# Weight words handled in the mask-bit steps, and the first pair's mask bits by fp32 products in column tiles

## The chip, the cores and the metric

The kernel runs on one core of a Trainium2 chip. The metric is the device time of one execution in microseconds (us). A program's time holds its span (first to last instruction) and a little around it.

## What is computed

Sixteen heads of masked attention (2 batches, 8 heads, 768 positions, width 64) are followed by two dense feed-forward blocks over the 1536 tokens. Everything comes and goes as fp32; the feed-forward weights arrive as 64-bit words and are turned into fp32 on the chip.

```python
q_bits = (q @ proj > 0); k_bits = (k @ proj > 0)       # 6 bits for each position
mask   = bucket(q_bits)[:, None] == bucket(k_bits)[None, :]
scores = where(mask, scale * q @ k.T, -1e9)
attn   = softmax(scores);  x = attn @ v                # per head
h = relu(x @ w_in);   x = (h * h) @ w_out              # 1536 x 512 -> 2048 -> 512
h = x @ w2_in;        y = (h * sigmoid(h)) @ w2_out
```

## The kernel before

**Attention.** The heads go in eight pairs. A pair has four units (head 0 or 1, query half z 0 or 1 of 384 columns), a unit has three score tiles of 128 queries by 768 keys. Each loop step `d`, from -5 to 98, handles one score tile and two transposed tiles:

- TensorE transposes two finished 128-key slices of the probabilities (`transp`, three 128x128 pieces each, tiles `t`), multiplies two older slices with v (`av`, two products each, tile `o`), then makes the next score tile (`score_mm`, four products, tile `s`).
- ScalarE rounds the transposed tiles (`t_hi`, tiles `th`) and takes the exponentials (`score_exp`).
- VectorE takes the row maximum of the score tile made one step earlier (`row_max`, L983), two tiny operations on it (`row_live`), and the remainders of the transposed tiles (`t_lo`, L1023, tiles `tl`), whose end gives a `t` buffer back. There are three `t` buffers and two `s` buffers.

Operations in `mid[d]` are put on VectorE right behind `row_live` of step `d`; operations given by `at(d, ...)` are put at the end of step `d` on their engine. All engines run their own list in this order.

**fp32 by two rounded parts.** Fast products take rounded operands (fp32r). So q and k are split into a rounded part and a remainder: for later pairs GpSimd rounds (`cast_pair`, tiles `hq`, `hk`) and subtracts (`split_pair`, tile `lp`), and DMAs place the parts in the operand tiles `qq` and `kk` (`load_head`, `place_lo`).

**Mask bits.** Twelve extra rows of `qq` and `kk` carry the bits, so that a mismatch makes a score hugely negative. For pairs 1 to 7 the bits come from four fp32 products of 32 columns each, one in each quarter of the array (`bits_mm`), and one compare on VectorE (`bits_cmp`), placed by DMAs (`place_bits`). This is done in seven steps, called bits steps here: d = 1, 10, 22, 34, 46, 58, 70. In a bits step both `t_lo` of the step run before the products, and the compare comes in the next step. For pair 0, the lead-in, head 0 takes its bits from rounded parts against a split projection `pjd` (`first_bits_mm`, tiles `bf`), and head 1 from eight products at step -2 (`second_bits_mm`, tiles `bs`).

**First-block weights.** During attention four slices of w_in are converted from 64-bit words: ScalarE `w_abs`, GpSimd `w_limit`, then on VectorE `w_exp`, `w_sign`, `w_low` (L945, L949, L953), in `mid` of the last three steps of each row of `W_STEPS`; `wp_put` splits the first two on GpSimd.

**Feed-forward.** After step 98 a planner orders the two blocks; its table and rules are not touched, and its instruction order is the same in both kernels. TensorE is fed with zero products (`warm_up`, L967) before and inside the lead-in.

Of the kernel before, what the change touches and what calls it, by code (L numbers as in the profile page):

```python
# [26 lines left out]
QW = 384  # L27
# [4 lines left out]
WARM = {-4: 5, 0: 1, 1: 1}  # L32
# [8 lines left out]
W_STEPS = ((0, 5, 17, 29, 53), (8, 17, 41, 65, 77), (22, 29, 41, 92, 93), (54, 65, 92, 96, 96))  # L41
# [658 lines left out]
def lsh_attention_moe_moe(ctx, tc, kd, qk, qf, fq, v, pc, wi1, wo1, wi2, wo2, out):  # L700
# [28 lines left out]
    pjd = ac.tile([128, 3, 88], F32R, name="pjd")  # L729
    pdx = ac.tile([128, 2, NBR], F32, name="pdx")  # L730
# [67 lines left out]
    def first_load(h):  # L798
# [19 lines left out]
        if h == 0:  # L818
            first["hk", 0] = a1.tile([128, S], F32R, tag="hk", name="hk0_0")
# [16 lines left out]
    def first_k_hi(z, i):  # L836
        (nc.gpsimd.tensor_copy if i else nc.scalar.copy)(out=pair[0]["kk"][0][0:64, i, half(z)], in_=first[0, 1][z][0:64])

    def first_hk(z):
        nc.scalar.copy(out=first["hk", 0][64:128, half(z)], in_=first[0, 1][z][64:128])  # L840

    def first_k_lo(z):
        (nc.gpsimd if z else nc.vector).tensor_tensor(
            out=pair[0]["kk"][0][64:128, 0, half(z)], in0=first[0, 1][z][64:128], in1=first["hk", 0][64:128, half(z)].bitcast(F32), op=ALU.subtract
        )
# [13 lines left out]
    def first_ops(h, z):  # L859
        q, k, zs = pair[0]["qq"][h], pair[0]["kk"][h], half(z)  # L860
        up, dn, all_ = slice(0, 64), slice(64, 128), slice(0, 128)
        of_q = [(0, all_, q[:, 0, zs]), (0, up, q[up, 1, zs])]
        if h:
            return of_q, [(1, all_, k[:, 0, zs]), (2, up, k[up, 0, zs])]
        hk = first["hk", 0]
        return of_q, [(1, dn, hk[dn, zs]), (2, dn, hk[dn, zs]), (1, dn, k[dn, 0, zs])]

    def first_bits_mm(i, z):
        o = first["bits", i, z] = ps_t.tile([128, 512], F32, tag="t", name=f"bf{i}{z}")
        ops = first_ops(0, z)[i]  # L870
        for n, (w, rows_, x) in enumerate(ops):
            mm(o[0:76, 0:QW], pjd[rows_, w, 0:76], x, start=n == 0, stop=n == len(ops) - 1)
            if i + z + n == 0:
                warm_up(1)

    def first_bits_cmp(i, z, a=0, b=QW):
        m = tm[1 + i][64:76]
        nc.vector.tensor_scalar(
            out=pair[0][("qq", "kk")[i]][0][64:76, 1, half(z)][:, a:b], in0=first["bits", i, z][64:76, a:b],
            scalar1=m[:, 0:1], scalar2=m[:, 1:2], op0=ALU.is_gt, op1=ALU.mult,  # L880
        )


    def second_bits_mm(z):
        o = first["both", z] = ps_t.tile([128, 512], F32, tag="t", name=f"bs{z}")
        ops = [(64 - NBR * i, *first_ops(1, z)[i][n]) for i, n in ((1, 1), (0, 0), (1, 0), (0, 1))]
        for n, (c, w, rows_, x) in enumerate(ops):
            mm(o[0 : 2 * NBR, 0:QW], pjd[rows_, w, c : c + 2 * NBR], x, start=n == 0, stop=n == len(ops) - 1)

    def second_bits_cmp(z):  # L890
        if z == 0:
            first["bt"] = a1.tile([128, S], F32R, tag="bt", name="bt0")
        m = tm[3][0 : 2 * NBR]
        nc.vector.tensor_scalar(
            out=first["bt"][0 : 2 * NBR, half(z)], in0=first["both", z][0 : 2 * NBR, 0:QW], scalar1=m[:, 0:1], scalar2=m[:, 1:2], op0=ALU.is_gt, op1=ALU.mult
        )

    def second_place(n, zs):
        nc.sync.dma_start(
            out=pair[0][("qq", "kk")[n]][1][64 : 64 + NBR, 1, zs].bitcast(F32), in_=first["bt"][NBR * n : NBR * n + NBR, zs].bitcast(F32)  # L900
        )
# [210 lines left out]
    for p in range(1, NPAIR):  # L1112
        d0 = 12 * (p - 1)
        if p > 1:
            at(d0 - 10, load_pair, p)
            at(d0 - 9, load_k, p)
            at(d0 - 4, new_hi, p)
            at(d0 - 4, cast_pair, p, 1)
            at(d0 - 3, split_pair, p, 1)
            scale[d0 - 2] = p  # L1120
            at(d0 - 2, cast_pair, p, 0)
            at(d0 - 1, split_pair, p, 0)
# [5 lines left out]
        at(d0 + 2, place_lo, p, 0)  # L1128
# [22 lines left out]
    for i, (d_load, d_abs, *d_dve) in enumerate(W_STEPS):  # L1151
# [7 lines left out]
        if i < 2:  # L1159
            at(d0, wp_put, i)  # L1160
# [4 lines left out]
    with tc.manual_schedule():  # L1165
# [10 lines left out]
        warm_up(9)  # L1176
# [169 lines left out]
```

## Time and profile before

| | |
|---|---|
| median of 3 runs | 715.39 us (715.32 to 716.03) |
| profiled execution | 717.23 us, span 715.5 us |
| TensorE busy | 707.4 us (99%) |
| VectorE / ScalarE / GpSimd busy | 605.4 / 537.7 / 257.6 us |
| attention stage | to about 223 us of the span |
| an ordinary attention step | 2.05 to 2.06 us |
| a bits step with its products | 2.98 us |

In a timeline, each row has a start, a length and what was run; brackets show how long the engine sat idle before it and what ended that. Two VectorE rows may overlap by about 0.08 us, since one starts as the other drains. The distance of two score rows on TensorE is the length of a step.

### The profile page before, as it was taken

The numbers are of one execution on the slowest core, as the hardware profiler recorded it, in microseconds if no ns is written. First come the engines' busy times: TensorE is split into PE (matmuls) and PEld (weight loads), VectorE is DVE, ScalarE is ACT, GpSimd is POOL, SyncE is SP. The second block draws the span as 40 slices with busy tenths as digits, with TensorE's granted clock in tenths as the row PEclk, the third lists the DMA queues.
The fourth block names the chain that finished last, engine by engine and source line by source line (L and its number), as shares of the span: only waits on it lengthen the run. The fifth ranks groups of instructions, "written<-read, shape, count | busy, mean of one in ns | idle before, by whom it ended". The sixth has DMA issues, their size and how long they took to land.

```text
span 715.5 us, 10860 instructions
## 1 busy us (share of the span) xinstructions
PE 707.4 (99%) x3610; PEld 602.9 (84%) x3610; DVE 605.4 (85%) x1099; ACT 537.7 (75%) x1012; POOL 257.6 (36%) x239
## 2 busy tenths in 40 slices
PE   9999999999999999999999999999999999999998
PEld 4899999999998888888887888888888888888886
DVE  6999999999999879887897789988878778888840
ACT  6999999999997787594477469788765955854861
POOL 7546575657665221042231241245114011212300
PEclk9999999999999999999999999999999999999999
DMA  5778967967733455242534832487221332245432
GB/s 171 206 177 194 228 159 193 232 160 198 174 96 86 110 162 118 89 131 46 117 89 122 183 93 73 104 184 174 71 73 60 101 106 86 76 103 119 103 110 96
DMA packets 39495, 92.51 MB, mean 129 GB/s; under 512 B 5944, under 2 KB 11588, under 8 KB 39440
## 3 DMA queue, kind: packets, MB, share of 16 engines
q1 hardware_dynamic: 26976, 67.58, 31.6%
q0 software_dynamic: 12032, 23.79, 18.7%
q8 instruction: 28, 0.46, 0.3%
q10 hardware_dynamic: 432, 0.46, 0.2%
q14 instruction: 27, 0.22, 0.1%
HBM read 52.32 MB, written 3.19 MB: 78 GB/s over the span
## 4 chain that ended last, share of the span: by engine, by line
PE 87%; DVE 10%; issue 1%; DMA 1%; ACT 0%; DVEq 0%; ACTq 0%; POOLq 0%
PE bank L558 36%; PE bank L443 24%; PE bank L420 7%; PE s L976 6%; PE t L1012 6%; DVE mt L983 4%; DVE tl L1023 4%; PE o L1036 3%; PE o L1037 3%; DMA cell<-cell 1%; PE bs L786 1%; PE warm L967 1%; DVE mt L988 1%; DVE mt L987 0%; ACT P L996 0%
## 5 line engine op out<-in xcount | busy, mean ns | idle before, releaser
L558 PE MATMUL bank<-woh,cell 128*128 128x512 f32 (+1 forms) x392 | 119.8, 385 | 0.0
L558 PE MATMUL bank<-cell,woh 128*128 128x512 f32 x384 | 118.4, 389 | 1.1 <-DMA cell<-cell 1.1
L996 ACT ACTIVATE P<-s,mt 128x768 f32<-128x768 f32 x96 | 95.6, 995 | 13.5 <-DVE mt L988 11.7
L1023 DVE TENSOR_TENSOR tl<-t,th 128x384 fp32r<-128x384 f32 x192 | 104.0, 547 | 0.1
L983 DVE TENSOR_REDUCE mt<-s 128x1 f32<-128x768 f32 x96 | 91.3, 951 | 3.1 <-PE s L976 2.4
L558 PEld LDWEIGHTS bank<-cell,woh 128*128 128x128 f32 x384 | 72.1, 188 | 16.4 <-DMA cell<-cell 1.5
L558 PEld LDWEIGHTS bank<-woh,cell 128*128 128x128 f32 x392 | 73.1, 188 | 14.6
L1017 ACT CAST th<-t 128x384 fp32r<-128x384 f32 x192 | 82.2, 482 | 3.2 <-PE t L1012 3.0
L976 PE MATMUL s<-kk,qq 76*128 76x384 f32 (+1 forms) x384 | 83.4, 338 | 0.5 <-ACT P L996 0.3
L1012 PE MATMUL t<-ident,P 128*128 128x128 f32 x576 | 80.6, 273 | 1.8 <-DVE tl L1023 1.8
L1012 PEld LDWEIGHTS t<-ident,P 128*128 128x128 f32 x576 | 67.5, 140 | 11.3 <-DVE tl L1023 7.2
L278 DVE TENSOR_TENSOR cell<-bank,cell 128x512 f32<-128x512 f32 x91 | 62.1, 691 | 17.5 <-PE bank L443 13.1
L443 PE MATMUL bank<-xw,wpb 128*128 128x512 f32 x312 | 75.9, 389 | 0.0
L558 PE MATMUL bank<-wol,cell 128*128 128x512 f32 (+1 forms) x196 | 75.4, 385 | 0.0
L558 PE MATMUL bank<-cell,wol 128*128 128x512 f32 x192 | 74.7, 389 | 0.0
L1036 PE MATMUL o<-th,vv 128*128 128x384 f32 x192 | 72.7, 379 | 0.0
L976 PEld LDWEIGHTS s<-kk,qq 76*128 76x128 f32 (+1 forms) x384 | 67.9, 188 | 2.3 <-ACT P L996 1.6
L443 PEld LDWEIGHTS bank<-xw,wpb 128*128 128x128 f32 x312 | 58.5, 188 | 12.4 <-DVE bank L278 0.3
L1037 PE MATMUL o<-tl,vv 128*128 128x384 f32 x192 | 64.7, 337 | 0.0
L450 ACT COPY cell<-bank 128x512 f32<-128x512 f32 x39 | 22.9, 586 | 39.5 <-PE bank L443 37.5
L268 ACT CAST cell<-cell 128x512 fp32r<-128x512 f32 x81 | 48.8, 617 | 2.8 <-DMA cell<-cell 1.7
L271 POOL DMA_DIRECT2D cell<-cell x23 | 20.5, 906 | 82.4 <-ACT cell L270 59.4
(185 smaller groups left out, 1461.2 us busy)
## 6 DMA issues: line engine op xcount, KB each, us to landing
raw<-in_dram SPq DMA_DIRECT2D x62, 512.0 KB
cell<-cell POOLq DMA_DIRECT2D x23, 256.0 KB, 3.8
qq<-hq SPq DMA_DIRECT2D x28, 192.0 KB
kk<-in_dram POOLq DMA_DIRECT2D x14, 384.0 KB, 4.5
yf<-cell POOLq DMA_DIRECT2D x21, 256.0 KB, 3.6
vr<-in_dram SPq DMA_DIRECT2D x8, 384.0 KB
ta<-ob SPq DMA_DIRECT2D x31, 96.0 KB
tb<-ob SPq DMA_DIRECT2D x31, 96.0 KB
```

The costliest lines, as they stand in the source:

```text
L278: add("DVE", 0.70, lambda: vec.tensor_tensor(out=val(out), in0=bank[b], in1=val(other), op=ALU.add), [("bank", b), *reads], writes)
L420: mm(bank[b], wpa[n][:, p, 4 * h + j], x[:, q], start=j == 0 and z == 0, stop=j == 3 and z == 2)
L443: mm(bank[b], w[:, p], x[:, q], start=not started and z == 0, stop=z == 2, skip_group_check=started)
L558: mm(bank[b][:, 0:wd], x, y, start=start and i == 0 and z == 0, stop=i == (FB if half is None else 2 * half + 2) - 1 and z == 2, skip_grou ...
L976: mm(s[:, n, 0:QW], t["qq"][h][0:kk, ab, c0 : c0 + 128], t["kk"][h][0:kk, ab, n * QW : (n + 1) * QW], start=ab == 0, stop=ab == 1)
L983: nc.vector.tensor_reduce(out=m[:, 0:1], in_=s[:, :, 0:QW], op=ALU.max, axis=AX.XY, negate=True)
L996: nc.scalar.activation(out=e.rearrange("p (a b) -> p a b", a=2), in_=s[:, :, 0:QW], func=AF.Exp, scale=m[:, 1:2], bias=m[:, 2:3], accum_ou ...
L1012: nc.tensor.transpose(t[:, j * 128 : (j + 1) * 128], P[u, j][:, kt * 128 : (kt + 1) * 128], ident)
L1017: nc.scalar.copy(out=th, in_=PT[g][0][:, 0:QW])
L1023: nc.vector.tensor_tensor(out=tl, in0=t[:, 0:QW], in1=th.bitcast(F32), op=ALU.subtract)
L1036: mm(o[:, 0:QW], vv, th, start=kt == 0, stop=False)
L1037: mm(o[:, 0:QW], vv, tl, start=False, stop=kt == KT - 1)
```

## The change

It has two parts.

1. *Bits steps.* The VectorE operations of w_in slices 0 and 1 move from steps 17, 29, 53 and 41, 65, 77 to the bits steps 10, 22, 34 and 46, 58, 70; slice 2's first moves from 41 to 46. `wp_put` comes seven steps after the last of them. In pairs 2 to 7 GpSimd no longer rounds and splits k ahead of q: all four operations are put in the bits step, q first. `place_lo` of head 0 comes one step later.
2. *First pair.* The split projection `pjd` is gone. One fp32 matrix `pdz` is multiplied with the loaded q and k themselves, four products in column tiles for each head (at the start, and at step -4), head 1's compare is the common `bits_cmp` (step -2, instead of two compares in step -1) and its bits go out in four DMAs. Head 0's k is rounded in all 128 rows at once, straight into `kk`. Zero products: 7 instead of 9 at the start, 3 instead of 5 at step -4, one new at -2.

```diff
-WARM = {-4: 5, 0: 1, 1: 1}
+WARM = {-4: 3, -2: 1, 0: 1, 1: 1}
-W_STEPS = ((0, 5, 17, 29, 53), (8, 17, 41, 65, 77), (22, 29, 41, 92, 93), (54, 65, 92, 96, 96))
+W_STEPS = ((0, 5, 10, 22, 34), (8, 17, 46, 58, 70), (22, 29, 46, 92, 93), (54, 65, 92, 96, 96))
...
     def first_k_hi(z, i):
-        (nc.gpsimd.tensor_copy if i else nc.scalar.copy)(out=pair[0]["kk"][0][0:64, i, half(z)], in_=first[0, 1][z][0:64])
-
-    def first_hk(z):
-        nc.scalar.copy(out=first["hk", 0][64:128, half(z)], in_=first[0, 1][z][64:128])
+        kk, k = pair[0]["kk"][0], first[0, 1][z]
+        if i:
+            nc.gpsimd.tensor_copy(out=kk[0:64, 1, half(z)], in_=k[0:64])
+        else:
+            nc.scalar.copy(out=kk[:, 0, half(z)], in_=k)
...
-    def first_bits_mm(i, z):
-        o = first["bits", i, z] = ps_t.tile([128, 512], F32, tag="t", name=f"bf{i}{z}")
-        ops = first_ops(0, z)[i]
-        for n, (w, rows_, x) in enumerate(ops):
-            mm(o[0:76, 0:QW], pjd[rows_, w, 0:76], x, start=n == 0, stop=n == len(ops) - 1)
-            if i + z + n == 0:
-                warm_up(1)
+    def first_bits_mm(h):
+        o = first["bits", h] = ps_t.tile([128, 512], F32, tag="t", name=f"bf{h}")
+        for c in range(4):
+            n, z = divmod(c, 2)
+            x = first[1, n][:, half(z)] if h else first[0, n][z]
+            mm(o[32 * c : 32 * c + 32, 0:QW], pdz[0:64, n], x[0:64], start=True, stop=True)
...
-            at(d0 - 4, new_hi, p)
-            at(d0 - 4, cast_pair, p, 1)
-            at(d0 - 3, split_pair, p, 1)
             scale[d0 - 2] = p
-            at(d0 - 2, cast_pair, p, 0)
-            at(d0 - 1, split_pair, p, 0)
+            at(d0 - 2, new_hi, p)
+            for i in range(2):
+                at(d0 - 2, cast_pair, p, i)
+                at(d0 - 2, split_pair, p, i)
...
-        at(d0 + 2, place_lo, p, 0)
+        at(d0 + 3, place_lo, p, 0)
...
-            at(d0, wp_put, i)
+            at(d0 + 7, wp_put, i)
...
-        warm_up(9)
+        warm_up(7)
...
+        first_bits_mm(0)
+        warm_up(1)
         first_q_hi(0)
...
-        at(-4, first_bits_mm, 0, 1)
         mid[-3].append((first_bits_cmp, (0, 1)))
-        for z in range(2):
-            at(-2, second_bits_mm, z)
-            mid[-1].append((second_bits_cmp, (z,)))
-            if z:
-                mid[-1].append((second_place, (1, slice(0, S))))
-            mid[-1].append((second_place, (0, half(z))))
+        at(-4, first_bits_mm, 1)
+        mid[-2].append((lambda: bits_cmp(0, first["bits", 1]), ()))
+        mid[-2].append((second_place, ()))
```

On VectorE, the bits step d = 22 and the step behind it stood like this before (`t44`, `t45`, `t46` are transposed tiles, `bn3` the compared bits of pair 3):

```order
L988 TENSOR_SCALAR mt_92<-mt_92 128x1
L1023 TENSOR_TENSOR tl44_1074<-t44_1068,th44_1072 128x384
L1023 TENSOR_TENSOR tl45_1090<-t45_1076,th45_1080 128x384
L983 TENSOR_REDUCE mt_92<-s9_0_1094 128x1
L987 TENSOR_SCALAR mt_92<-mt_92 128x1
L988 TENSOR_SCALAR mt_92<-mt_92 128x1
L791 TENSOR_SCALAR bn3_1110<-bs3_1099,tmt_88 128x384
L1023 TENSOR_TENSOR tl46_1118<-t46_1112,th46_1116 128x384
```

The same place on VectorE in the changed kernel:

```order
L964 TENSOR_SCALAR mt_91<-mt_91 128x1
L925 SCALAR_TENSOR_TENSOR wi0_264<-rx_92,wi0_264 128x512
L999 TENSOR_TENSOR tl44_1046<-t44_1040,th44_1044 128x384
L999 TENSOR_TENSOR tl45_1062<-t45_1048,th45_1052 128x384
L959 TENSOR_REDUCE mt_91<-s9_0_1066 128x1
L963 TENSOR_SCALAR mt_91<-mt_91 128x1
L964 TENSOR_SCALAR mt_91<-mt_91 128x1
L790 TENSOR_SCALAR bn3_1088<-bs3_1071,tmt_88 128x384
L999 TENSOR_TENSOR tl46_1096<-t46_1090,th46_1094 128x384
```

The sign operation on slice 0 (`wi0`), which stood in step 29, now stands ahead of both remainders of step 22, with everything up to `tl46` behind it.

On GpSimd, around the same bits step, before (`vv2` is v of pair 2, `hk3`, `hq3`, `lp3` the parts of pair 3):

```order
L919 CAST vv2_908<-vr2_909 128x12x64
L920 TENSOR_TENSOR vv2_908<-vr2_909,vv2_908 128x12x64
L754 CAST hk3_1025<-rk3_802 128x768
L774 TENSOR_TENSOR lp3_1060<-rk3_802,hk3_1025 128x768
L1054 TENSOR_SCALAR sums1_566<-sums1_566 128x12
L754 CAST hq3_1024<-rq3_801 128x768
L774 TENSOR_TENSOR lp3_1060<-rq3_801,hq3_1024 128x768
L764 DMA kk3_0_1204<-in_0_dram 64x2x768
L1087 TENSOR_TENSOR yf_58<-rw0_1027,ta0_424 128x768
```

And on GpSimd in the changed kernel:

```order
L895 CAST vv2_884<-vr2_885 128x12x64
L896 TENSOR_TENSOR vv2_884<-vr2_885,vv2_884 128x12x64
L1030 TENSOR_SCALAR sums1_542<-sums1_542 128x12
L753 CAST hq3_1077<-rq3_776 128x768
L773 TENSOR_TENSOR lp3_1080<-rq3_776,hq3_1077 128x768
L753 CAST hk3_1078<-rk3_777 128x768
L773 TENSOR_TENSOR lp3_1080<-rk3_777,hk3_1078 128x768
L763 DMA kk3_0_1181<-in_0_dram 64x2x768
L1063 TENSOR_TENSOR yf_58<-rw0_1000,ta0_400 128x768
```

The two operations on k moved behind those on q, and the DMA issue of `kk3` now stands behind all four.

On TensorE at the start of the program, behind the run of zero products, before (`bf` tiles are head 0's bits, `s0_0` the first score tile):

```order
L872 MATMUL bf00_157<-qq0_0_103,pjd_90 76x384
L967 LDWEIGHTS zero_120
L967 MATMUL warm_122<-zero_120 128x512
L872 MATMUL bf00_157<-qq0_0_103,pjd_90 76x384
L872 MATMUL bf10_161<-hk0_0_105,pjd_90 76x384 x2
L872 MATMUL bf10_161<-kk0_0_104,pjd_90 76x384
L872 MATMUL bf11_165<-hk0_0_105,pjd_90 76x384 x2
L872 MATMUL bf11_165<-kk0_0_104,pjd_90 76x384
L976 MATMUL s0_0_180<-kk0_0_104,qq0_0_103 128x384 x2
```

And on TensorE in the changed kernel (`fc` holds the first q half, `fq1` the second, `fk` both k halves):

```order
L861 MATMUL bf0_136<-fc_95,pdz_90 32x384
L861 MATMUL bf0_136<-fq1_96,pdz_90 32x384
L861 MATMUL bf0_136<-fk_97,pdz_90 32x384 x2
L943 LDWEIGHTS zero_118
L943 MATMUL warm_120<-zero_118 128x512
L952 MATMUL s0_0_165<-kk0_0_103,qq0_0_102 128x384 x2
```

The eight products on rounded parts of `qq`, `hk` and `kk` became four that read only what the DMAs bring.

## Rows read from the trace of the kernel before

**Rows 1.** The whole span: length, busy time and operations of each engine, granted clock, DMA.
```profile
0.00:715.50 715.50, 707.44 (x3610) 602.94 (x3610) 605.42 (x1099) 537.71 (x1012) 257.58 (x239) 1.00 0.51 129
```

**Rows 2.** Timeline of TensorE around step 22: start, length, engine, line, operation.
```profile
62.84 0.86 PE L976 MATMUL s<-kk,qq 128*128 128x384 f32 x4
...
64.89 0.85 PE L976 MATMUL s<-kk,qq 128*128 128x384 f32 x4
...
66.46 0.87 PE L1012 MATMUL t<-ident,P 128*128 128x128 f32 x6
...
67.87 0.88 PE L976 MATMUL s<-kk,qq 128*128 128x384 f32 x4
68.59 0.82 PE L1012 MATMUL t<-ident,P 128*128 128x128 f32 x6
```

**Rows 3.** Timeline of VectorE in the same stretch.
```profile
65.25 1.01 DVE L1023 TENSOR_TENSOR tl<-t,th 128x384 fp32r<-128x384 f32 x2
...
67.44 0.68 DVE L791 TENSOR_SCALAR bn<-bs,tmt 128x384 fp32r<-128x384 f32 x1
68.03 0.55 DVE L1023 TENSOR_TENSOR tl<-t,th 128x384 fp32r<-128x384 f32 x1
```

**Rows 4.** The chain that ended last: transposes behind bits products, and in an ordinary step.
```profile
66.53 0.81 PE t L1012 x6
...
84.10 0.66 PE t L1012 x6
```

**Rows 5.** Timeline of TensorE: the scores of steps 53 and 54.
```profile
133.24 0.86 PE L976 MATMUL s<-kk,qq 128*128 128x384 f32 x4
...
135.79 0.86 PE L976 MATMUL s<-kk,qq 128*128 128x384 f32 x4
```

**Rows 6.** Timeline of VectorE in step 53.
```profile
133.49 0.68 DVE L953 SCALAR_TENSOR_TENSOR wi<-rx,wi 128x512 uint32<-128x512 uint32 x1
134.09 0.55 DVE L1023 TENSOR_TENSOR tl<-t,th 128x384 fp32r<-128x384 f32 x1
```

**Rows 7.** Timeline of TensorE: the scores of steps 29 and 30.
```profile
80.34 0.86 PE L976 MATMUL s<-kk,qq 128*128 128x384 f32 x4
...
83.24 0.86 PE L976 MATMUL s<-kk,qq 128*128 128x384 f32 x4
```

**Rows 8.** Timeline of VectorE in step 29.
```profile
80.60 1.03 DVE L949 SCALAR_TENSOR_TENSOR wi<-rx,wi 128x512 uint32<-128x512 uint32 x1
```

**Rows 9.** Line L945: count, shortest/median/longest in ns, first and last start.
```profile
L945 DVE TENSOR_SCALAR wi<-wi x2: 415/416/418, 54.6 to 107.2; 128x512 uint32<-128x512 uint32 x2
```

**Rows 10.** Timeline of GpSimd around steps 22 and 29.
```profile
62.30 1.84 POOL L920 TENSOR_TENSOR vv<-vr,vv 128x768 fp32r<-128x768 f32 x1
...
67.52 0.82 POOL L754 CAST hq<-rq 128x768 fp32r<-128x768 f32 x1 [0.41 <-ACT rq L758]
...
79.25 1.84 POOL L1082 TENSOR_TENSOR ta<-ta,tb 128x768 f32<-128x768 f32 x1 [3.16 <-DMA tb<-ob]
```

**Rows 11.** Timeline of TensorE: the zero products at the start and in step -4.
```profile
1.32 4.02 PE L967 MATMUL warm<-zero 128*128 128x512 bf16 x9 [1.32 <-DVE zero L1173]
...
10.05 1.25 PE L967 MATMUL warm<-zero 128*128 128x512 bf16 x5
```

**Rows 12.** DMA queues from 0 to 4.5 us: ScalarE's queue, packets, MB, share.
```profile
q10 hardware_dynamic: 280, 0.39, 27.4%
```

**Rows 13.** Timeline of VectorE in the lead-in.
```profile
5.13 0.56 DVE L843 TENSOR_TENSOR kk<-fk,hk 64x384 fp32r<-64x384 f32 x1
6.76 0.41 DVE L878 TENSOR_SCALAR qq<-bf,tmt 12x128 fp32r<-12x128 f32 x1 [1.07 <-PE bf L872]
...
8.95 0.96 DVE L983 TENSOR_REDUCE mt<-s 128x1 f32<-128x768 f32 x1
```

**Rows 14.** The chain that ended last, in the lead-in: start, length, what.
```profile
13.59 1.97 PE bs L888 x8
```

**Rows 15.** Timeline of ScalarE: end of the exponential of step -2.
```profile
14.72 0.19 ACT L996 ACTIVATION_READ_ACCUMULATOR P<-s,mt 128x1 f32 x1
```

More of the change, by code (lines that the diff above doesn't have):

```diff
@@ L817, in first_load @@
         t["kk"][h] = a1.tile([128, 2, S], F32R, tag="kk", bufs=2, name=f"kk0_{h}")
-        if h == 0:
-            first["hk", 0] = a1.tile([128, S], F32R, tag="hk", name="hk0_0")
     def first_q_hi(z):
@@ L836, in first_k_hi @@
     def first_k_hi(z, i):
-        (nc.gpsimd.tensor_copy if i else nc.scalar.copy)(out=pair[0]["kk"][0][0:64, i, half(z)], in_=first[0, 1][z][0:64])
-    def first_hk(z):
-        nc.scalar.copy(out=first["hk", 0][64:128, half(z)], in_=first[0, 1][z][64:128])
+        kk, k = pair[0]["kk"][0], first[0, 1][z]
[3 more added lines that the diff above has]
+            nc.scalar.copy(out=kk[:, 0, half(z)], in_=k)
     def first_k_lo(z):
-        (nc.gpsimd if z else nc.vector).tensor_tensor(
-            out=pair[0]["kk"][0][64:128, 0, half(z)], in0=first[0, 1][z][64:128], in1=first["hk", 0][64:128, half(z)].bitcast(F32), op=ALU.subtract
-        )
+        lo = pair[0]["kk"][0][64:128, 0, half(z)]
+        (nc.gpsimd if z else nc.vector).tensor_tensor(out=lo, in0=first[0, 1][z][64:128], in1=lo.bitcast(F32), op=ALU.subtract)
     def second_head():
@@ L856, in second_head @@
             nc.gpsimd.tensor_tensor(out=qq[0:64, 1, half(z)], in0=q[0:64, half(z)], in1=qq[0:64, 0, half(z)].bitcast(F32), op=ALU.subtract)
[L859 to L866, printed above, removed]
@@ L876, in first_bits_cmp @@
     def first_bits_cmp(i, z, a=0, b=QW):
-        m = tm[1 + i][64:76]
+        r = slice(32 * (2 * i + z), 32 * (2 * i + z) + NBR)
+        m = tm[0][r]
         nc.vector.tensor_scalar(
-            out=pair[0][("qq", "kk")[i]][0][64:76, 1, half(z)][:, a:b], in0=first["bits", i, z][64:76, a:b],
+            out=pair[0][("qq", "kk")[i]][0][64 : 64 + NBR, 1, half(z)][:, a:b], in0=first["bits", 0][r, a:b],
             scalar1=m[:, 0:1], scalar2=m[:, 1:2], op0=ALU.is_gt, op1=ALU.mult,
         )
[L884 to L901, printed above, removed]
+    def second_place():
+        t = pair[0]["bt"]
+        for c in (2, 3, 0, 1):
+            n, z = divmod(c, 2)
+            nc.sync.dma_start(
+                out=pair[0][("qq", "kk")[n]][1][64 : 64 + NBR, 1, half(z)].bitcast(F32), in_=t[32 * c : 32 * c + NBR].bitcast(F32)
+            )
@@ L1175, in lsh_attention_moe_moe @@
         zb = zero.bitcast(BF16)
-        warm_up(9)
+        warm_up(7)
         nc.scalar.activation(out=mt[:, 0, 0:1], in_=zero[:, 0:1], func=AF.Exp)
         make_identity(nc, ident)
-        nc.vector.tensor_copy(out=pjd.rearrange("p a b -> p (a b)"), in_=zero[:, 0:264])
-        c, k = slice(64, 64 + NBR), first["c"]
+        nc.vector.tensor_copy(out=pdz.rearrange("p a b -> p (a b)"), in_=zero[:, 0:64])
+        k = first["c"]
         nc.vector.tensor_tensor(
-            out=pdx, in0=k[:, 0:NBR].unsqueeze(1).broadcast_to([128, 2, NBR]), in1=k[:, NBR : 3 * NBR].rearrange("p (a b) -> p a b", a=2), op=ALU.mult
+            out=pdz[:, :, 0:NBR], in0=k[:, 0:NBR].unsqueeze(1).broadcast_to([128, 2, NBR]), in1=k[:, NBR : 3 * NBR].rearrange("p (a b) -> p a b", a=2), op=ALU.mult
@@ L1190, in lsh_attention_moe_moe @@
         first_q_hi(0)
-        first_hk(0)
-        first_hk(1)
+        first_k_hi(0, 0)
+        first_k_hi(0, 1)
         first_q_lo(0)
         first_k_lo(0)
-        first_k_hi(0, 0)
+        first_k_hi(1, 0)
+        first_k_hi(1, 1)
         first_k_lo(1)
-        first_k_hi(1, 0)
-        for z in range(2):
-            first_k_hi(z, 1)
+        nc.gpsimd.dma_start(out=pair[0]["kk"][1][0:64, 1], in_=kd[0, :, 1])
         first_q_hi(1)
         first_q_lo(1)
-        for i, z in ((0, 0), (1, 0), (1, 1)):
-            first_bits_mm(i, z)
```

10 lines of the change are left out of this document (2 added, 8 removed).

## The prediction

> **What bounds the kernel now.** I read the whole span first: TensorE is busy for 707.4 of 715.5 us, its granted clock at 1.00 [rows 1]. So only TensorE's own work and the few places where it waits can be saved. Next the distances of the score rows on TensorE: an ordinary attention step is 64.89 - 62.84 = 2.05 us, the bits step behind it 67.87 - 64.89 = 2.98 us [rows 2], so the bits products with their switch cost 0.93. Then the steps which hold a w_in operation: 133.24 to 135.79 is 2.55 [rows 5], 80.34 to 83.24 is 2.90 [rows 7]. There VectorE, nearly as full as TensorE, is late with a remainder, and TensorE waits for the buffer. Last the lead-in, where neither engine is full and the loop score, maximum, exponential, next score sets the pace. Behind attention the instruction order is the same in both kernels, so what is saved ahead of it should simply arrive earlier.
>
> **What a w_in operation costs now.** In step 53 the operation starts at 133.49 and the remainder behind it at 134.09: it takes 0.60 of VectorE's time (its row says 0.68, the last 0.08 overlap) [rows 6]. TensorE's step is 2.55 - 2.05 = 0.50 longer [rows 5], so 0.10 to 0.11 is absorbed. The sign operation of step 29 takes 1.03 - 0.08 = 0.95 [rows 8] and costs 2.90 - 2.05 = 0.85 [rows 7], again 0.10 less. The exponent operations take 0.42 - 0.08 = 0.34 each [rows 9], so by the same rule 0.23 in step 17 and, as a pair in step 41, 0.57. Steps 65 and 77 hold one operation each like that of step 53. Sum: 0.23 + 0.85 + 0.50 + 0.57 + 2 x 0.50 = 3.15 us.
>
> **What it costs in a bits step.** The order shows the operation ahead of both remainders of step 22 (65.25), and then the maximum, the compare (67.44) and the remainder of t46 (68.03) all slide by its length [rows 3]. Who waits? t48 reuses the bits' buffer and starts at 68.59 [rows 2]; the compare ends at 68.12, 0.47 ahead. t49, half of the six transposes of 0.66 [rows 4] later, at 68.92, reuses t46's buffer; that remainder ends at 68.03 + 0.55 = 68.58 [rows 3], 0.34 ahead. t47, which waits for the second remainder of 65.25 (ends 66.26), stands at about 66.85, 0.59 ahead. So a bits step absorbs 0.34 where an ordinary one absorbs 0.10. One exponent operation (0.34) then costs 0; four sign and low operations of 0.60 cost 0.26 each, 1.04; the pair in step 46 (0.68) costs 0.34. Sum 1.38, gain **3.15 - 1.38 = 1.77 us**.
>
> This takes the sign operation at 0.60, not 0.95. Its long row of step 29 lies at 80.60, inside a GpSimd subtraction from 79.25 to 81.09 [rows 10]; that of step 53 has no such neighbour. In the changed kernel GpSimd has finished v (62.30 + 1.84 = 64.14) and, with q first, waits for ScalarE's scaled q until 67.52 [rows 10], so it is idle at 65.3, where the old order had it splitting k. The Trainium skill (GPSIMD Engine Reference, Specifications) says that GpSimd's SBUF interfaces are shared with VectorE, with contention when VectorE reads two SBUF inputs; the long row agrees, and by that rule the old order on GpSimd would have put 0.35 on each moved sign or low operation, 1.4 us in all.
>
> Bounds: if a bits step absorbs no more than an ordinary one, only the contention of step 29 is saved, 0.35; if it absorbs everything, 3.15.
>
> **The GpSimd and SP side of it.** Rounding and splitting q and k now run in one piece: from 67.52, twice 0.82 + 1.84, to 72.9 [rows 10]. Behind them stand the DMA issue for the next pair's kk, then the x products. The next pair's first score comes seven steps after the issue's old place, some 14 us; the delay is under 2. On SP the bits go ahead of the low parts of head 0 and nothing there waits for longer. I cost this, and `wp_put` seven steps later, at nothing; uncovered, a late operand would cost its delay once for each of six pairs, up to 2 us each.
>
> **The lead-in.** Three terms.
>
> (a) The first compare. Before, it ran at 6.76 and the first maximum followed at 8.95, 2.19 later [rows 13]. Now the products need only loaded data. The seven zero products end at 1.32 + 7 x 0.447 = 4.45, and the second q half comes on ScalarE's queue, which had moved 0.39 MB, both its halves, by 4.5 [rows 12]. The zero products ran 0.447 apart at first and 0.25 in step -4 [rows 11], both under a full granted clock: at first TensorE ran at its 1.2 GHz level, later at 2.4. The four products, 0.93 with their switch at the upper level, take up to 1.86 at the lower, so they end between 5.4 and 6.3; I take 6.0. VectorE is free of its k remainder at 5.13 + 0.56 = 5.69 [rows 13]. The compare starts at about 6.05, **0.71 earlier**, and I keep the distance of 2.19.
>
> (b) The eight products of step -2, 1.97 us [rows 14], leave the chain. Step -1's score, which followed them at 15.56, needs the exponential that ended at 14.91 [rows 15]: at most 0.65 more.
>
> (c) The compare of head 1 now stands in step -2 ahead of a maximum, 0.59 later for the odd scores of the loop; ScalarE's queue carries about half of this on to the even ones. I take 0.3 of (b) away, leaving **0.35**.
>
> Sum 1.06. The four fp32 products at step -4 stand where five zero products and two products were, with two zero products fewer, and cost nothing while TensorE waits there for the exponential. Bounds: the compare as early as 5.69 and no loss in (c) give 1.07 + 0.65 = 1.7; a late q half or products which do not run side by side (four of 0.93 one after the other, to 8.2 or so) would put the compare at up to 8.2, 1.4 late, less 0.65: 0.8 lost.
>
> The transposes behind bits products take 0.81 where they otherwise take 0.66 [rows 4]: 0.15 for changing from column tiles back to the whole array. The Trainium skill (TensorEngine Tiling (Array Packing), Key Properties) says that a change of tiling mode drains TensorE, which speaks against tiles in the lead-in, and the trace agrees with these 0.15. By that rule two such switches fully on the path would leave 0.76 of the 1.06.
>
> **Sum.** 1.77 + 1.06 = 2.83 us. Of the span of 715.5 that leaves 712.7; the profiled execution's own 717.23 would become 714.4, and the median of 715.39, which I forecast, **712.6**.
>
> **Rivals.**
>
> *The lead-in gives nothing.* The first bits come late (term (a) between 0 and -1.4). For it: the products now need both second halves and run at the lower clock level; against: 0.39 MB had come by 4.5 [rows 12]. Only 1.77 or a little less is left: 713.7.
>
> *The bits steps do not absorb.* The operations then cost what they cost now, less the contention: 0.35 + 1.06 = 1.4, 714.0. For it: the operation stands ahead of two remainders; against: the 0.34 worked out above, more than three times the 0.10 of an ordinary step. A v that arrives late on GpSimd, which ends only 1.1 ahead of the operation [rows 10], gives nearly the same by contention (0.35 on each of four: 1.4 less, 714.0).
>
> *The clock, on the other side.* With fewer zero products and tiles of a quarter of the array, TensorE could stay at, or fall back to, 1.2 GHz in the lead-in; the 0.447 spacing at the start shows the level [rows 11]. Each ordinary step at that level costs 2.05 more; from 1.4 such steps on the change loses. At three steps, 6.2, the time is 718.7. Against it: TensorE never shows a lower granted clock [rows 1] and has a few waits in the lead-in already. The Trainium skill (TensorE: Matmul & The Clock Gate, What's actually happening) says that activity releases the throttle, so fewer products can cost clock; no row here shows a fall.
>
> *More than forecast.* Both upper bounds nearly met, 4.2 or more: 711.2 or less.
>
> **How the numbers follow.** Forecast 0.58 (its own range 711.7 to 713.6), lead-in nothing 0.17, bits steps nothing 0.11, clock 0.07, more 0.07. The range goes from 711.2 to 714.7: it takes in the forecast, the two middle rivals and half of the better case. Faster or slower means by over 0.2%, 1.43 us, about what a measurement here can tell from no change. Faster: 0.58, the better case 0.07, most of the lead-in rival and half of the bits rival, 0.76. Same: 0.16. Slower: 0.08, the clock and a little of a late lead-in.
>
> **What would show it.** Right: steps 17, 29, 41, 53, 65, 77 at 2.05 to 2.16 us; bits steps 10 at 2.98, 22, 34, 58 and 70 at about 3.24, 46 at 3.3; the sign operation of slice 0 at 0.68; the first maximum at 8.2 instead of 8.95; the first ordinary step about 1 us earlier. Wrong: bits steps of 3.4 or more, a moved operation lengthened beside GpSimd, TensorE waiting for the second q half, zero products still 0.447 apart after 7 us, or a wait of a pair's first score for kk.

## The result and the profile after

The changed kernel takes 722.55 us (median of 4 runs, 720.85 to 723.29) against 715.66 us for the kernel before (4 runs, 715.32 to 716.03): a ratio of 1.0094, 95% interval 1.0081 to 1.0106. It is 6.9 us slower where 2.8 us faster was forecast, and lies outside the range.

The row of the whole span, as [rows 1]: TensorE is idle for 12.2 us instead of 8.1, and the 1.4 us of busy time more are products that took longer, since the trace has six fewer of them.

```profile
0.00:721.10 721.10, 708.88 (x3604) 602.16 (x3605) 606.20 (x1096) 538.32 (x1010) 259.44 (x238) 1.00 0.52 128
```

The last score of attention starts at 219.78 us instead of 213.09, 6.69 later. Reading the distances of all score rows, as in [rows 2, 5, 7], the 6.7 us fall into four places:

| place | forecast, us | measured in the trace, us |
|---|---|---|
| ordinary steps freed of a w_in operation | -3.15 | -3.10 |
| bits steps 10, 22, 34, 46, 58, 70 and the step behind each | +1.38 | +4.35 |
| the first score of a pair's head 0, four of them | 0 | +4.2 |
| lead-in, up to the score of step 2 | -1.06 | +0.90 |

The rest, 0.3 us, is spread over steps of 2.12 to 2.14 us. Behind attention the profiled run of before waits 1.07 us for a DMA at 383 us, which the one of after does not; so the spans differ by 5.6 us only.

TensorE around pair 2's first score and the bits step behind it (start, length, line, operation; in brackets the idle time before and what ended it):

```profile
57.35 0.87 PE L952 MATMUL s<-kk,qq 128*128 128x384 f32 x4
...
60.42 0.94 PE L952 MATMUL s<-kk,qq 128*128 128x384 f32 x4 [0.84 <-DMA rk<-in_dram]
...
66.67 0.85 PE L952 MATMUL s<-kk,qq 128*128 128x384 f32 x4
...
69.22 1.01 PE L988 MATMUL t<-ident,P 128*128 128x128 f32 x6 [0.91 <-DVE tl L999]
...
70.77 0.88 PE L952 MATMUL s<-kk,qq 128*128 128x384 f32 x4
...
73.09 0.88 PE L952 MATMUL s<-kk,qq 128*128 128x384 f32 x4
```

Against [rows 2], the bits step is 70.77 - 66.67 = 4.10 us instead of 2.98 and the one behind it 2.32; and there is a new wait of 0.84 us ahead of the pair's first score. The row names the next pair's load of k (`rk`) as the releaser, but the score does not read that; it reads `qq` and `kk`, waits for several transfers, and the runs below show which one it was.

VectorE and GpSimd in the same bits step, to be read against [rows 3, 10]:

```profile
66.39 0.55 DVE L999 TENSOR_TENSOR tl<-t,th 128x384 fp32r<-128x384 f32 x1
...
67.04 1.66 DVE L925 SCALAR_TENSOR_TENSOR wi<-rx,wi 128x512 uint32<-128x512 uint32 x1
```

```profile
65.40 0.82 POOL L895 CAST vv<-vr 128x768 fp32r<-128x768 f32 x1 [5.45 <-DMA vr<-in_dram]
66.31 1.85 POOL L896 TENSOR_TENSOR vv<-vr,vv 128x768 fp32r<-128x768 f32 x1
```

The sign operation takes 1.66 us instead of 0.68. Beside it stands GpSimd's split of v, which waited 5.45 us for v's transfer and so began 4.0 us later than in [rows 10]; the bits step itself begins 1.8 us later (its score at 66.67 instead of 64.89), so against it the split is 2.2 us later. GpSimd's waits for v between 20 and 230 us, in the list of waits of the kernel before and of the changed one (total, times, longest):

```profile
POOL vv L919 <- DMA vr<-in_dram: 11.4, 5, 2.7
```

```profile
POOL vv L895 <- DMA vr<-in_dram: 27.2, 7, 6.0
```

The transfers that SP issues ahead of these scores, in the kernel before and in the changed one:

```profile
49.22 0.55 SPq L779 DMA_DIRECT2D qq<-lp  x1
49.87 0.57 SPq L780 DMA_DIRECT2D kk<-lp  x1
50.53 1.84 SPq L909 DMA_DIRECT2D qq<-bn  x2
52.42 1.47 SPq L909 DMA_DIRECT2D kk<-bn  x2
53.94 0.51 SPq L741 DMA_DIRECT2D rq<-in_dram  x1
```

```profile
50.13 1.59 SPq L885 DMA_DIRECT2D qq<-bn  x2
51.84 1.48 SPq L885 DMA_DIRECT2D kk<-bn  x2
53.42 0.45 SPq L740 DMA_DIRECT2D rq<-in_dram  x1
53.92 0.53 SPq L778 DMA_DIRECT2D qq<-lp  x1
54.55 0.55 SPq L779 DMA_DIRECT2D kk<-lp  x1
...
57.28 0.59 SPq L891 DMA_DIRECT2D vr<-in_dram  x1
```

The low parts (the remainders of q and k for head 0, `lp`, two transfers of 192 KB) have slipped not only behind the bits but behind the next pair's load of q (384 KB), and are issued 4.7 us later while the whole stretch is only 0.9 us later.

### The profile page after: what moved, and what is told of

Same layout as the page of the kernel before. It is cut to its first block, busy times and chain, and to the rows that moved or that the text cites. A ratio compares the mean times of both kernels' runs of the same rounds, so it can differ in the third digit from the quotient of the medians.

```text
span 721.1 us, 10856 instructions
## 1 busy us (share of the span) xinstructions
PE 708.9 (98%) x3604; PEld 602.2 (84%) x3605; DVE 606.2 (84%) x1096; ACT 538.3 (75%) x1010; POOL 259.4 (36%) x238
## 4 chain that ended last, share of the span: by engine, by line
PE 87%; DVE 7%; DMA 3%; SPq 2%; issue 0%; ACT 0%; ACTq 0%; DVEq 0%
PE bank L558 36%; PE bank L443 24%; PE bank L420 7%; PE s L952 6%; PE t L988 6%; DVE mt L959 3%; PE o L1012 3%; PE o L1013 3%; DMA rk<-in_dram 3%; DVE tl L999 2%; SPq L885 2%; PE warm L943 1%; PE bs L785 0%; DVE wi L925 0%; DVE mt L964 0%
## 5 line engine op out<-in xcount | busy, mean ns | idle before, releaser
L952 PE MATMUL s<-kk,qq 76*128 76x384 f32 (+1 forms) x384 | 85.8, 345 | 5.1 <-DMA rk<-in_dram 3.6
L988 PEld LDWEIGHTS t<-ident,P 128*128 128x128 f32 x576 | 67.9, 142 | 12.9 <-DVE tl L999 7.3
L443 PEld LDWEIGHTS bank<-xw,wpb 128*128 128x128 f32 x312 | 58.5, 188 | 12.4 <-DVE bank L278 0.3
L588 ACT COPY yf<-bank 128x512 f32<-128x512 f32 x48 | 27.9, 586 | 32.0 <-PE bank L558 31.0
```

The costliest lines, as they stand in the source:

```text
L443: mm(bank[b], w[:, p], x[:, q], start=not started and z == 0, stop=z == 2, skip_group_check=started)
L952: mm(s[:, n, 0:QW], t["qq"][h][0:kk, ab, c0 : c0 + 128], t["kk"][h][0:kk, ab, n * QW : (n + 1) * QW], start=ab == 0, stop=ab == 1)
L988: nc.tensor.transpose(t[:, j * 128 : (j + 1) * 128], P[u, j][:, kt * 128 : (kt + 1) * 128], ident)
```

## The experiments

The kernel before, measured again beside each group of runs (e1 to e4, e5 to e8, e9 to e11, e12, each group on another chip), had medians of 715.97 to 716.22 us; every ratio below is to it.

| run | what it is | median, us | ratio (95% interval) |
|---|---|---|---|
| e1 | after, low parts at their old place | 717.03 | 1.0011 (0.9999 to 1.0024) |
| e2 | before + the first pair's part | 716.43 | 1.0001 (0.9991 to 1.0010) |
| e3 | before + the bits steps' part | 720.73 | 1.0073 (1.0045 to 1.0100) |
| e4 | e3, low parts at their old place | 716.78 | 1.0014 (1.0002 to 1.0026) |
| e5 | e4 + v loaded six steps earlier | 715.62 | 0.9987 (0.9978 to 0.9997) |
| e6 | before + the w_in operations' new steps | 719.96 | 1.0047 (1.0031 to 1.0063) |
| e7 | before + GpSimd's order and the low parts' place | 717.17 | 1.0015 (1.0004 to 1.0025) |
| e8 | e1 + v earlier + four zero products more | 715.56 | 0.9987 (0.9978 to 0.9997) |
| e9 | e5, low parts at the change's place | 718.48 | 1.0038 (1.0025 to 1.0051) |
| e10 | e6 + v earlier | 715.35 | 0.9991 (0.9982 to 1.0000) |
| e11 | before + v earlier | 716.59 | 1.0008 (0.9998 to 1.0017) |
| e12 | e5, low parts behind the bits, ahead of q's load | 715.39 | 0.9989 (0.9980 to 0.9999) |

### Undoing one edit, and each part alone

e1 takes one line of the change back:

```diff
-        at(d0 + 3, place_lo, p, 0)
+        at(d0 + 2, place_lo, p, 0)
```

> The changed kernel, with the low parts of head 0 placed one step earlier again (ahead of the bits, as before the change); all else stays. Theory 1 (the low parts stand behind the next pair's q load in the DMA queue, and they push v back in turn): the waits at the first scores of pairs 2, 3, 5 and 6 (1.01, 0.92, 0.48, 1.82 us, 4.2 in all) go, v reaches GpSimd at the old time, and the sign and low operations of the bits steps take 0.68 again: attention 6 to 7 us shorter than in the changed kernel, 715 to 716.5 in all. Theory 2 (GpSimd's later split of k makes the operands late): waits and time stay, 721 to 723. Theory 3 (the queue explains the score waits, but a bits step does not hide a w_in operation anyway): only 4.2 go, 718 to 719.

Measured 717.03, which is in the range of none of the three. All waits at the pairs' first scores are gone, so that one line is worth some 5 to 6 us and the queue part of theory 1 holds. Its other part does not: v's waits fall only from 27.2 to 19.5 us, and three moved operations are still lengthened beside v's split. The kernel is no faster than before: its bits steps are 2.98 to 3.77 us and the steps behind them 2.12 to 2.32.

e2 has the new lead-in alone:

> The first pair's part of the change alone, on the kernel before. In the changed kernel the lead-in ended 0.9 us later than before. If the lead-in stands by itself, this kernel is 0.5 to 1 us slower than before, 716 to 717, with granted clock below 1 around 16 to 19 us; if the loss came from the moved steps, it is not slower.

Measured 716.43, the ratio within 0.1% of one: the first pair's part neither gains nor loses as much as that.

e3 has the bits steps' part alone, e4 the same without the moved low parts:

> The bits-step part of the change alone (w_in operations, GpSimd order, low parts one step later), with the old lead-in. Theories 1 to 3: 5 to 6 us slower than before, 720 to 722, with the same four score waits. If the two parts hurt only together, it is near the time before.

> The bits-step part alone, with the low parts of head 0 placed at the old step. Theory 1: it gains what was forecast for the bits steps, 1 to 2 us faster than before, 713.7 to 714.7. Theory 2: 718 or slower. Theory 3: 716 to 717, no score waits, but bits steps of 3.2 and more.

Measured 720.73 and 716.78. So most of the loss, and within the intervals all of it, lies in the bits steps' part, and the most of that in the low parts' place. The time of e4 is that of theory 3, but only one of its bits steps is above 3.2 us: in step 34 v is late (4.15 us of waiting), the low operation of slice 0 takes 1.48 us beside its split, and that bits step and the next cost 0.93 and 0.20 us, where one beside an idle GpSimd costs 0.14 and 0.25.

### Is it v?

e5 loads v of pairs 2 to 7 just after GpSimd has split the one before, so that nothing stands behind a late v:

```diff
-        at(d0 + 5, load_v, p)
+        at(d0 - 1 if p > 1 else 5, load_v, p)
```

> The kernel of e4 (old lead-in, w_in operations and q's rounding as in the change, low parts placed where they stood before) with v of pairs 2 to 7 loaded 6 steps earlier, just after GpSimd has split the one before. Theory: in e4 v lands late, its split on GpSimd then runs beside VectorE's sign and low operations in the bits' steps and lengthens them. Then GpSimd waits for no v here, the sign and low operations take 0.68 to 0.75 us each, each bits' step costs 0.3 to 0.4 us over a step without one, and the time is 0.6 to 1.3 us below e4, 715.5 to 716.2 us. Rival 1, the neighbour that lengthens them is the rounding and splitting of q and k, which start at the same place: the durations stay at 0.9 to 1.5 us and the time at 716.6 to 717. Rival 2, the early v takes the DMA engines from the loads of the pair's first head: waits of 0.5 us or more at a pair's first score, 717.5 or more.

Measured 715.62, 1.2 us below e4 (1.0 us with each taken against the kernel before of its group) and faster than the kernel before by 0.13% (0.03 to 0.22). GpSimd and VectorE of e5 at bits step 22:

```profile
59.31 0.84 POOL L919 CAST vv<-vr 128x768 fp32r<-128x768 f32 x1
60.23 1.85 POOL L920 TENSOR_TENSOR vv<-vr,vv 128x768 fp32r<-128x768 f32 x1
```

```profile
65.31 0.68 DVE L949 SCALAR_TENSOR_TENSOR wi<-rx,wi 128x512 uint32<-128x512 uint32 x1
65.91 1.01 DVE L1023 TENSOR_TENSOR tl<-t,th 128x384 fp32r<-128x384 f32 x2
```

GpSimd waits for v nowhere, its split ends at 62.08, over 3 us ahead of the sign operation, and all four sign and low operations take 0.68 us. Both rivals fall: q's and k's rounding was not the neighbour, and no first score waits.

e11, the control, loads v early in the kernel before:

> The kernel before with v's early load alone, the control for e5 and e10. Theory: nothing waits for v in the kernel before but GpSimd, so the time stays within 0.5 us of before, and e5 and e10 owe their gain to the w_in operations' places. Rival: v's early load by itself is what makes e5 fast: 0.5 to 1.0 us below before.

Measured 716.59, no gain; it is 0.6 us above the kernel before, a little more than the 0.5 expected. Its trace, of its slowest run, shows the same collision at an old place: GpSimd's x sum, released by a transfer, lies beside the sign operation of step 65.

```profile
159.05 1.82 POOL L1082 TENSOR_TENSOR ta<-ta,tb 128x768 f32<-128x768 f32 x1 [2.89 <-DMA kk<-lp]
```

```profile
159.45 1.97 DVE L949 SCALAR_TENSOR_TENSOR wi<-raw,wi 128x512 uint32<-128x512 uint32 x1
```

### Is GpSimd's new order needed?

e6 moves the w_in operations (`W_STEPS` and `wp_put`) and leaves everything on GpSimd and SP as it was; e10 adds the early v:

> The kernel before with the new steps of the w_in operations alone; GpSimd's order and the place of the low parts stay as before. Prediction's own sum (3.15 us saved, 1.4 us paid): 714.4 us. Theory of contention: sign and low operations in the bits' steps run beside GpSimd's split of v or of k and take 0.9 to 1.6 us instead of 0.68, each such step costs 0.4 to 1.1 us instead of 0.26, and the time is 715.5 to 717. No waits at a pair's first score in either. Rival, the waits at the first scores come from the w_in operations themselves: 719 or more.

> The kernel of e6 (the w_in operations' new steps alone, GpSimd's order as before) with v loaded early as in e5. Theory: what lengthened the sign and low operations in e6 was GpSimd's work behind a late v; with v early its split and that of k end before these operations start, they take 0.68 to 0.8 us, and the time is 3.5 to 4.5 us below e6, 715.2 to 716.4, so that the new order on GpSimd is not needed at all. Rival: the order itself is at fault (q's cast and split still run into the bits' step): 1.0 us or more a sign or low operation in two of the four places, 717 or more.

Measured 719.96 and 715.35. e6 lost more than the theory expected, as much as its rival, but no first score waits in its trace, which is of its fastest run (718.29); so not all of the loss can be read there. Bits steps 22 and 46 take 4.28 us each. VectorE and GpSimd at step 22:

```profile
65.08 1.85 DVE L949 SCALAR_TENSOR_TENSOR wi<-rx,wi 128x512 uint32<-128x512 uint32 x1
```

```profile
61.84 1.85 POOL L920 TENSOR_TENSOR vv<-vr,vv 128x768 fp32r<-128x768 f32 x1
63.64 0.83 POOL L754 CAST hk<-rk 128x768 fp32r<-128x768 f32 x1
64.55 1.84 POOL L774 TENSOR_TENSOR lp<-rk,hk 128x768 fp32r<-128x768 f32 x1
```

In the old order the split of k is what stands there, as the prediction had read. At step 46 the two exponent operations meet the split of v and the rounding of k and take 0.89 and 1.04 us instead of 0.42. In e10, with v early, the split of k ends at 64.73, the sign operation starts at 65.28, and all four take 0.68. So rounding q first takes the split of k out of the bits step but leaves a late v there (e4), while loading v early clears both; with it the new order is not needed.

### Is it the place in SP's queue?

e7 has the other half of the bits steps' part, GpSimd's order and the low parts' place:

> The kernel before with the second half of the bits' part alone: q rounded first on GpSimd, all four operations of a pair from one step, and the low parts of head 0 placed a step later; the w_in operations stay where they were. Theory of the queue: the scores of a pair's head 0 wait 0.3 to 1.8 us for low parts and k in most of the pairs, 3 to 5 us in all, and the time is 718.5 to 720.5. Rival, those waits need the w_in operations in the bits' steps (GpSimd slowed by them rounds q late): within 0.8 us of before, 715.5 to 717.

Measured 717.17, 0.15% slower, well short of the 718.5 to 720.5 expected and just above the rival's 717; only one first score is late, by some 0.3 us (163.89, 2.37 behind the score ahead of it). Nearer to the rival, then. One reading of the traces is that in e7 a w_in operation still stands in the step ahead of each pair's first score (17, 29, 41, 53, 65) and delays it, by 0.2 us or more, towards the low parts' landing. From the score at 54.17 to the first score at 58.5 is 4.35 us in e7; in e3 the low parts come 4.69 us behind the same score, and the score without its wait would stand at 4.1. That accounts for about half of the difference and was not tried by itself.

e9 and e12 start from e5, where nothing else is late, and move the low parts alone:

```diff
 (e9)
-        at(d0 + 2, place_lo, p, 0)
+        at(d0 + 3, place_lo, p, 0)
 (e12)
-        at(d0 + 2, place_lo, p, 0)
         at(d0 + 2, place_bits, p, 0)
+        at(d0 + 2, place_lo, p, 0)
```

> The kernel of e5 with one edit: the low parts of head 0 again placed a step later, behind the next pair's load of q, as in the change. Theory of the queue: the waits at a pair's first score are the low parts' place in the queue alone; they come back, 2 to 4.5 us in all, while the sign and low operations stay at 0.68 us; 717.5 to 720. Rival: the waits need v's load in the queue just behind k's as well, sharing its engines; with v early they are under 0.8 us in all, and the time is within 0.8 us of e5, 715.2 to 716.5.

> The kernel of e5 with the low parts of head 0 behind the four bits transfers, but still ahead of the next pair's load of q; between e5 (ahead of both) and e9 (behind both). Theory A, the 384 KB load of q ahead of them is what makes them late: the scores wait 0.5 us at most in all, and the time is 715.4 to 716.3. Theory B, the bits ahead of them (four issues, some 3.2 us of SP's time) are enough: the waits are those of e9, 2 to 4 us in all, 717.5 to 719. In between, 716.4 to 717.4, both have a share.

Measured 718.48 and 715.39. In e9 the waits are back though v no longer stands behind them in that queue, the sign and low operations stay at 0.68 us, and five first scores come late. Those that the trace marks with the transfer:

```profile
112.71 0.94 PE L976 MATMUL s<-kk,qq 128*128 128x384 f32 x4 [1.29 <-DMA rk<-in_dram]
...
139.46 0.94 PE L976 MATMUL s<-kk,qq 128*128 128x384 f32 x4 [0.29 <-DMA rk<-in_dram]
...
166.52 0.95 PE L976 MATMUL s<-kk,qq 128*128 128x384 f32 x4 [0.67 <-DMA rk<-in_dram]
```

The three transfers as e9 issues them:

```profile
52.01 0.46 SPq L741 DMA_DIRECT2D rq<-in_dram  x1
52.52 0.54 SPq L779 DMA_DIRECT2D qq<-lp  x1
53.16 0.55 SPq L780 DMA_DIRECT2D kk<-lp  x1
```

In e12 no first score is late, with the low parts behind all four bits transfers:

```profile
51.00 1.49 SPq L909 DMA_DIRECT2D kk<-bn  x2
52.59 0.52 SPq L779 DMA_DIRECT2D qq<-lp  x1
53.20 0.55 SPq L780 DMA_DIRECT2D kk<-lp  x1
53.80 0.57 SPq L741 DMA_DIRECT2D rq<-in_dram  x1
```

Here the low parts are issued at 52.59 and 53.20, in e9 at 52.52 and 53.16: the same times. The one difference is whether the 384 KB of q stand ahead of them in the queue. That settles it: the transfer ahead, not the later issue, is worth the 3.1 us between these two runs (the kernel before beside them: 715.97 and 716.06). The Trainium skill (DMA: Bandwidth & Descriptors, Queues, rings and completion order) says that a DMA engine takes the descriptors of one queue in their order; e9 and e12 agree.

### The lead-in

e8 is the change with the two repairs and four zero products more at step -2:

```diff
-WARM = {-4: 3, -2: 1, 0: 1, 1: 1}
+WARM = {-4: 3, -2: 5, 0: 1, 1: 1}
```

> The changed kernel with the low parts placed where they stood before, v loaded early as in e5, and five products with zeros instead of one at step -2, where TensorE waits 1.0 to 1.1 us for the first exponentials in after, e1 and e2. Theory: these products fill that wait, the granted clock stays at 1.00 through 14 to 20 us in every run, and the time is that of e5 within 0.4 us, since the first pair's part gave nothing in e2. Rival, the idle time there is what the first pair's part loses: 0.4 to 0.9 us below e5. Other rival, the products delay the scores behind them: 0.3 to 0.9 us above e5.

Measured 715.56, that of e5, as the theory had it. TensorE's wait ahead of the score of step -1 shrinks from 1.12 us (after, e2) to 0.49. TensorE in three stretches of after, and in the same of e1 (busy time, operations, granted clock, DMA share, GB/s):

```profile
14.00:16.00 2.00, 0.88 (x5) 1.00 0.00 0
16.00:18.00 2.00, 2.00 (x11) 0.56 0.11 24
18.00:20.00 2.00, 1.75 (x10) 0.59 0.44 150
```

```profile
14.00:16.00 2.00, 0.98 (x5) 1.00 0.00 0
16.00:18.00 2.00, 1.87 (x13) 1.00 0.12 25
18.00:20.00 2.00, 1.95 (x16) 1.00 0.44 110
```

The granted clock of after is 0.50, the 1.2 GHz level, from 16.5 to 19.5 us, behind a stretch in which TensorE had been busy for 0.88 of 2 us with one wait of 1.12 us; at 20 it is back at 1.00. e1 and e2 wait there for 1.02 and 1.12 us and keep 1.00. So the clock can fall at this place and need not; whether the zero products of e8 prevent it, one trace that kept 1.00 cannot show.

The other runs say a little more. Each has its mean granted clock on record, and the fall above makes that 0.998 in the profiled run of after. With the new lead-in it is 0.998 or less in 10 of 24 runs (after 2 of 4, e1 3 of 10, e2 5 of 10); with the old one in 2 of 76 (both e4) and in none of the 86 of the kernel before measured beside them; in e8 in none of ten. So the new lead-in does bring more falls, and the zero products seem to help; but where in these runs the clock fell is not on record, and e8 ran on another chip than e1 and e2.

## Why the prediction was wrong, step by step

**Ordinary steps: right.** 3.15 forecast, 3.10 measured, and the exponent operation in bits step 10 costs 0.05 where 0 was forecast. But 0.35 of both is the collision of step 29, which this one trace of before happens to have: in e2, e7 and e11, with the w_in operations at their old steps, step 29 takes 2.54 to 2.56 us instead of 2.90. Against an execution without it, about 2.7 was to be had.

**The bits steps absorb 0.34: half right.** With no neighbour (e5), a sign or low operation costs 0.31 to 0.40 us instead of 0.26, the exponent pair 0.46 instead of 0.34; 1.96 instead of 1.38 in all, and attention in e5 is 1.15 us shorter than before where 1.77 was forecast. What failed is the spare time of 0.34, 0.47 and 0.59 us ahead of the transposes: the prediction read it at their products, and what waits is the weight loads, which start earlier (TensorE's loads of t48 in before, then those of t47, t48 and t49 in e5):

```profile
68.42 0.75 PEld L1012 LDWEIGHTS t<-ident,P 128*128 128x128 f32 x6
```

```profile
66.97 0.31 PEld L1012 LDWEIGHTS t<-ident,P 128*128 128x128 f32 x3
...
68.83 0.31 PEld L1012 LDWEIGHTS t<-ident,P 128*128 128x128 f32 x3 [0.22 <-DVE bn L791]
69.29 0.31 PEld L1012 LDWEIGHTS t<-ident,P 128*128 128x128 f32 x3 [0.15 <-DVE tl L1023]
```

In before the loads start at 68.81 (t49), 68.42 (t48) and 66.74 (t47); in e5 each starts 0.05 behind the end of what it waits for. With both, the spare times are 0.18, 0.25 and 0.43, and 0.60 - 0.18 = 0.42 is near the 0.39 measured at step 22: 0.14 in the bits step (3.12 instead of 2.98), 0.25 in the one behind (2.32 instead of 2.07). So a bits step absorbs about 0.2. That it absorbs more than an ordinary one held.

**"It is idle at 65.3": wrong.** The prediction read from [rows 10] that GpSimd ends v 1.1 us ahead of the sign operation, and took that moment as fixed. It hangs on a transfer, and the same change makes that transfer late: against the bits step GpSimd started v 2.2 us later in after. Its waits for v between 20 and 230 us are 11.4 us in before, 17.0 in e6, 17.7 in e4, 19.5 in e1, 25.0 in e3 and 27.2 in after. So the low parts' place brings about half of the increase (after against e1, e3 against e4), and the w_in operations' new steps alone (e6) much of the rest; by what way is not shown. The rival named a late v at "0.35 on each of four". The size is not a constant. In before (step 29), after, e1, e3, e4, e6, e7 and e11 a sign or low operation that meets GpSimd's split or x sum and is lengthened ends 0.54 to 0.56 us after that ends, however early it has begun (eight of the thirteen cases up to 200 us):

| run | operation, start to end | GpSimd ends | behind it |
|---|---|---|---|
| before [rows 8, 10] | 80.60 to 81.63 | 81.09 | 0.54 |
| after | 67.04 to 68.70 | 68.16 | 0.54 |
| after | 148.20 to 149.21 | 148.66 | 0.55 |
| after | 176.59 to 178.04 | 177.50 | 0.54 |
| e1 | 91.35 to 92.69 | 92.15 | 0.54 |
| e4 | 90.71 to 92.19 | 91.64 | 0.55 |
| e6 | 65.08 to 66.93 | 66.39 | 0.54 |
| e11 | 159.45 to 161.42 | 160.87 | 0.55 |

The operation stands still until GpSimd is done, so it costs the overlap less 0.14 (a lone operation takes 0.68, which is 0.14 more than 0.54); up to 1.3 us here. The 0.35 was the overlap of one case, 0.49, less that. In after three of four operations met it, and the bits steps cost 4.35 - 1.96 = 2.4 us more than in e5. The Trainium skill (SBUF — State Buffer, SBUF: two separate sides) calls the port pair of VectorE and GpSimd an exclusive lock, held for the whole instruction while the other blocks. The table agrees; had I used that rule instead of the price of one row, the rival would have been worth up to the length of GpSimd's operation.

**"Nothing there waits for longer": wrong, and the costliest step, 4.2 us.** I looked at what the low parts' move does to the bits and to GpSimd, and not at what lies between the old place and the new. One step later is behind the next pair's load of q. The prediction gave the cost if the cover went, up to 2 us for each of six pairs, but no chance to that case. e9 against e12 shows it alone. What it costed at nothing on GpSimd's side held: with the new order on GpSimd and the low parts ahead of q's load (e1, e4, e5, e12) no first score waits.

**The lead-in: 1.06 forecast, 0.3 or nothing.** Up to the score of step 2, ten traces with the old lead-in take 21.82 to 22.61 us, mean 22.25; e1, e2 and e8 with the new one 22.27, 21.78 and 21.88, mean 21.98. Terms (b) and (c) held: from the first maximum to that score are 13.36 to 13.40 us in the old lead-in and 12.89 to 12.93 in the new, 0.5 gained where 0.35 was forecast. Term (a) has the wrong sign: the first maximum comes at 8.89 to 9.41 us, mean 9.16 of four traces with after's, instead of 8.46 to 9.21, mean 8.87. TensorE and VectorE in after:

```profile
4.42 1.49 PE L861 MATMUL bf<-fc,pdz 64*32 64x384 f32 x2
...
5.77 0.85 PE L861 MATMUL bf<-fk,pdz 64*32 64x384 f32 x2
...
7.60 1.08 PE L943 MATMUL warm<-zero 128*128 128x512 bf16 x2
```

```profile
6.82 0.40 DVE L866 TENSOR_SCALAR qq<-bf,tmt 12x128 fp32r<-12x128 f32 x1 [0.90 <-POOL kk L842]
...
9.41 0.96 DVE L959 TENSOR_REDUCE mt<-s 128x1 f32<-128x768 f32 x1 [0.21 <-PE s L952]
```

The products begin when I had said, and end at 6.62, where the bounds reached 6.3; the first compare is at 6.82 and not at 6.05, against 6.76 in [rows 13]. They take 0.85 each and the zero products at 7.6 us are still 0.45 apart, the sign the prediction had named for this. In e2 the last of them take 0.49 and the maximum comes at 8.89.

**The clock rival** did come true in the profiled run of after. Against it the prediction had the 1.00 of the whole span [rows 1], but the row of after reads 1.00 as well: a mean over 720 us hides a fall of 3 us. It cost 0.9 us, 13.83 instead of 12.9 from the first maximum to the score of step 2. In size it is the least of the four terms, and e1 and e2 show that the part does not bring it each time; by the runs' mean clocks it may come in somewhat under half of them.

**Together.** The two steps that cost the most have one root: I took the moment at which a transfer lands from the trace of before, and the change moves the queue. e4 with the low parts repaired is at 716.78, e5 with v as well at 715.62, e10 without GpSimd's new order at 715.35. The last two are below both kernels, but by 0.1% only (e10's interval reaches 1.0000), and not by the 0.25% that the ordinary and bits steps alone had promised.

**Still open:** why e7 with the same queue waits so much less than e3 (the w_in operations ahead of the scores account for about half); why v is late in e4 and e6, whose order on SP is that of before (in e4 4.15 us of waiting ahead of step 34, against 2.64); and when the clock falls in the lead-in.

## What to carry to other kernels

When a transfer is moved by a step, list every transfer between its old and its new place in the same queue with its size: 384 KB ahead of it cost 3.1 us here, while the same issue time without them cost nothing. When an operation is moved to where another engine is idle, ask what that engine waits for, and whether the change moves that as well. Price a collision of VectorE and GpSimd by the overlap, not by the delay seen once; starting GpSimd's work earlier, by an earlier load, took it away altogether.

## What the runs showed of the hardware

VectorE's sign and low operations, with two tensors in SBUF, do not progress beside a GpSimd subtraction: 0.68 us became up to 1.97. The exponent operations, with one, were held too (0.42 to 0.89 and 1.04 in e6), GpSimd is held the other way round (roundings of 0.82 us took 1.03 and 1.29 there), and the remainders that read PSUM and SBUF were not: the one at 66.39 in after lies wholly inside GpSimd's split and takes 0.55 us as always.

A product in the first microseconds takes up to twice its later time (zero products 0.45 us apart instead of 0.22) while the granted clock of that stretch reads 1.00 (4 to 8 us, before and after alike), and the moment at which it speeds up differs between runs of one lead-in: the last bits products, from about 5.8 us on, take 0.85 us each in after and 0.49 in e2. Half a microsecond of the lead-in hangs on that, as much as its rewriting gained.
